# Attention feeding an ELU MLP on one core: q and k of each pair prepared two half slots sooner, and the first batch's x copied one half slot later

## The chip, the core and the metric

The kernel runs on one core of one Trainium2 chip. The metric is the device time of one execution in microseconds (us), given as the median of three runs.

The engines that matter here, by the names of the profile: PE (TensorE, matmuls), DVE (VectorE), ACT (ScalarE), POOL (GpSimd), and SP, whose queue issues every DMA of this kernel. Each engine takes its own instructions strictly in the order in which the program was written.

## What is computed

Eight batches of twelve heads, 448 positions, head size 64. q and k are RMS-normed with a gain, attention is plain softmax, and the heads of a batch are put side by side as x, which goes through a two-layer MLP with an ELU.

```python
def rmsnorm(x, g):
    rms = np.sqrt(np.mean(x * x, axis=-1, keepdims=True) + 1e-06)
    return x / rms * g
q_n, k_n = (rmsnorm(q, g_q), rmsnorm(k, g_k))
scores = scale * np.matmul(q_n, k_n.transpose(0, 1, 3, 2))
attn = softmax(scores)                       # max, exp, sum + 1e-9, divide
x = np.matmul(attn, v)                       # then (3584, 768)
h = x @ w_in                                 # 768 x 2048
g = np.where(h > 0.0, h, np.exp(np.minimum(h, 0.0)) - 1.0)
return g @ w_out                             # 2048 x 768
```

## The kernel before, in words

Heads are worked on in pairs, six pairs to a batch, 48 in all. A pair's 896 query rows are seven chunks of 128. Every float32 operand is split into a high and a low float16 part, so that a product is two or three float16 matmuls.

**Time is written out in half slots.** The main loop runs `h` from -18 to 699. A pair has `HP` = 14 half slots, a batch `HB` = 84. In an even half slot one chunk gets its row maximum (`s_max`, DVE, L542), the chunk before it its `s_z` (POOL, L552), the one before that its `s_hi` (ACT, L566). In an odd one there is `s_exp` (ACT, L548), `s_rec` (DVE, L559) and `s_lo` (DVE, L571). PE gets one chunk's score matmuls `s_mm` (L535) every two half slots, into four banks `s`; a bank is free again when that chunk's `s_lo` is done. `s_tr` (SP, L581) issues the DMA transposes of the attention weights, `pt<-gall` in the first batch and `pt<-p` later. At r = 7 of the next pair (r is the half slot inside a pair, `h` modulo 14) `attend` (PE, L592) multiplies them with v into the bank `av`, 22 matmuls. `x_high` (ACT, L599) and `x_low` (DVE, L603) then copy `av` into x.

**Everything else is a task hung on a half slot** by `at(h, fn, ...)`, and `run_tasks` writes out a half slot's tasks behind its softmax instructions. Thus a number in the table below decides where in each engine's queue an instruction stands, and nothing else. The order in which PE's instructions are written depends on those softmax steps, on the weights and on the MLP; the tasks moved here have none on PE.

**q and k of a pair** pass through `load_qk` (SP, DMA into `nat`), `qk_square` (ACT, L362), `qk_sum` (DVE, L366), `qk_root` (ACT, L370 and L371), `qk_newton` (DVE, L377 to L381), `qk_norm` (POOL, L391), `k_high` (ACT, L400), `q_gain` (POOL, L405), `q_high` (ACT, L410), `k_low` (POOL, L414), `q_low` (POOL, L421), two DMA transposes `qk_transpose` into `qkt` (SP, L429), and `q_swap` (SP, L436), two DMAs that put the halves of q the other way round. Only then can `s_mm` of the pair run. From the third pair on, `qk_square` writes its scratch into the `qkt` buffer that the next pair will fill.

**The weights** are split while the first two batches run: `conv_in` for sixteen blocks of `w_in` (load, two ACT steps L224 and L225 into `wts` and `w32s`, a DVE join L230 and sign L256, column sums on PE L129, POOL `whi` L282, PE L289 and L290, ACT `wli` L293), then `conv_out` for `w_out`. v has its own POOL steps (`v_mult`, `v_high` L448, `v_low` L453, `v_shift` L459).

The MLP's matmuls (L677, L691) start at h = 92, some seven to a half slot, and go on behind the attention's end. Its weights' low parts come from DRAM again for each batch (`wls`, L666), and batches from the third on have v read once more for its maximum (`vscan`, L162).

Of the kernel before, what the change touches and what calls it, by code (L numbers as in the profile page):

```python
# [20 lines left out]
NPAIR = H // 2  # L21
# [11 lines left out]
def tile_attention_then_elu_mlp(ctx: ExitStack, tc: tile.TileContext, qk, v, v_scan, gg, w_in, w_out, out):  # L33
# [668 lines left out]
    def at(h, fn, *args):  # L702
        tasks.setdefault(h, []).append((fn, args))
# [15 lines left out]
    }  # L719
    for p in range(NP):  # L720
        hb = HP * (p - 1)
        steps = (-20, -14, -12, -10, -8, -4, -1, -1, 1, 4, 2)
        steps = early.get(p) or [hb + h for h in steps]
        for h, fn in zip(steps, (
            load_qk, qk_square, qk_sum, qk_root, qk_newton, qk_norm, k_high, q_gain, q_high, k_low,
            q_low,
        )):

            at(-3 if p == 2 and fn == load_qk else h, fn, p)
        for h, i in ((4 if p > 1 else 6, 0), (6 if p > 1 else 8, 1)):  # L730
            at(hb + h, qk_transpose, p, i)
        at(hb + 8, q_swap, p)
        h0 = HP * p
        for h, fn in ((-2, load_v), (9, v_mult), (10, v_high), (11, v_low), (12, v_shift)):
            at(h0 + h + (5 if (p == 0) == (h > 0) and p < 2 else 0), fn, p)
        at(h0 + 22, x_high, p)
        at(h0 + 23, x_low, p)
    for b in range(B):
        h0 = HB * (b - 1) + (66 if b > 1 else 48) if b else -5
        for i in range(VSC):  # L740
# [27 lines left out]
    for h in range(H0, LAST):  # L768
# [28 lines left out]
        p, r = divmod(h, HP)  # L797
# [15 lines left out]
    h = LAST - 1  # L813
# [49 lines left out]
```

## Time and profile before

| | |
|---|---|
| three runs | 1286.1 us median, 1285.51 to 1286.39 |
| the profiled execution | 1287.73 us, of which 1285.6 us is the span from the first to the last instruction and 2.1 us lies around it |
| busy in the span | PE 1191.8 us (93%), ACT 878.7 (68%), DVE 853.3 (66%), POOL 529.4 (41%) |
| mean granted TensorE clock | 0.970 of full |
| DMA | 219.22 MB, nearly all issued by SP |

The profile gives one execution's instructions with start and duration. "Idle before <- releaser" is the time in which an engine did nothing ahead of an instruction, with what ended it. An engine's idle time matters where PE in turn waits for it.

### The profile page before, as it was taken

To read this page: it belongs to the slowest core of one execution; us is meant where nothing else is said; L and a number is where in the kernel's file an instruction comes from. 1 tells how busy PE (TensorE), PEld (TensorE's weight loads), DVE (VectorE), ACT (ScalarE), POOL (GpSimd) and SP (SyncE) were. 2 spreads that over 40 slices of the span, in tenths; PEclk is the share of its full clock that TensorE was granted. 3 is DMA by queue.
4 is the path that set the end of the run, shared out by engine and by line. 5 is a ranking of instruction groups with operands and counts; after the bars stand their busy time and mean duration, and the time that the engine had idled before them with its cause. 6 is when DMAs were issued, how large, how long until landed. Compare 5 with 4: busy or idle time off the path is not lost.

```text
span 1285.6 us, 21501 instructions
## 1 busy us (share of the span) xinstructions
PE 1191.8 (93%) x6976; PEld 716.4 (56%) x6976; DVE 853.3 (66%) x1913; ACT 878.7 (68%) x1889; POOL 529.4 (41%) x843
## 2 busy tenths in 40 slices
PE   3676578889999999999999999999999999999998
PEld 1333234456655765576556665576557755666576
DVE  7878779886677557856677567856785668642310
ACT  6887778985788558855797478855886578743520
POOL 3675775665334333343344433434334334420000
PEclk9878679999999999999999999999999999999999
DMA  8999898899877897889787986799787977663011
GB/s 274 224 215 239 199 224 181 199 205 236 175 147 154 203 197 142 164 166 223 149 164 157 215 176 148 155 197 203 139 169 166 219 152 171 133 147 87 1 47 62
DMA packets 452560, 219.22 MB, mean 171 GB/s; under 512 B 408673, under 2 KB 428769, under 8 KB 452449
## 3 DMA queue, kind: packets, MB, share of 16 engines
q1 hardware_dynamic: 452448, 217.86, 78.2%
q8 instruction: 55, 0.90, 0.3%
q14 instruction: 57, 0.46, 0.1%
HBM read 93.52 MB, written 14.16 MB: 84 GB/s over the span
## 4 chain that ended last, share of the span: by engine, by line
PE 79%; ACT 6%; DVE 5%; POOL 4%; issue 3%; DMA 2%; SPq 0%; ACTq 0%; POOLq 0%; DVEq 0%
PE mo L691 32%; PE mo L677 30%; PE s L535 8%; PE av L592 7%; DMA pt<-p 2%; PE mo L289 1%; ACT w32s L225 1%; ACT wts L224 1%; POOL nat L391 1%; ACT s L548 1%; POOL whi L282 1%; DVE wts L230 1%; DVE gall L571 1%; DVE st L542 1%; DVE gall L632 1%
## 5 line engine op out<-in xcount | busy, mean ns | idle before, releaser
L677 PE MATMUL mo<-x,whi 128*128 128x448 f16 x1536 | 422.8, 352 | 5.0 <-DVE e L624 5.0
L691 PE MATMUL mo<-gall,whos 128*128 128x448 f16 x1536 | 422.8, 353 | 0.7 <-DVE gall L632 0.7
L542 DVE TENSOR_REDUCE st<-s 128x1 f32<-128x448 f32 x336 | 208.4, 620 | 176.2 <-PE s L535 175.4
L552 POOL TENSOR_SCALAR st<-st 128x1 f32<-128x1 f32 x336 | 77.3, 230 | 552.4 <-ACT s L548 544.5
L691 PE MATMUL mo<-gall,wls 128*128 128x448 f16 x768 | 271.9, 354 | 0.0
L677 PE MATMUL mo<-x,wli 128*128 128x448 f16 x768 | 270.9, 353 | 0.0
L566 ACT ACTIVATE p<-s,st 128x448 f16<-128x448 f32 x294 | 185.6, 631 | 119.2 <-DMA pt<-p 99.9
L691 PEld LDWEIGHTS <-whos 128*128 128x128 f16 x1536 | 221.6, 145 | 72.3
L548 ACT ACTIVATE s<-s,st 128x448 f32<-128x448 f32 x336 | 203.2, 605 | 61.4 <-DVE st L542 58.4
L535 PE MATMUL s<-qkt 128*128 128x448 f16 (+1 forms) x768 | 188.8, 365 | 53.3 <-DVE gall L571 39.3
L677 PEld LDWEIGHTS <-whi 128*128 128x128 f16 x1536 | 150.2, 98 | 143.1 <-issue 6.9
L571 DVE SCALAR_TENSOR_TENSOR p<-s,st,p 128x448 f16<-128x448 f32 x294 | 196.4, 668 | 30.5 <-ACT p L566 28.5
L691 PEld LDWEIGHTS <-wls 128*128 128x128 f16 x768 | 110.4, 144 | 43.0 <-issue 8.4
L535 PEld LDWEIGHTS <-qkt 128*128 128x128 f16 (+1 forms) x768 | 63.2, 101 | 124.3 <-issue 62.4
L632 DVE SCALAR_TENSOR_TENSOR gall<-e,gsc,gall 128x448 f16<-128x448 f32 x128 | 100.8, 787 | 24.4 <-ACT gall L629 24.2
L677 PEld LDWEIGHTS <-wli 128*128 128x128 f16 x768 | 75.1, 98 | 74.7 <-issue 7.5
L592 PE MATMUL av<-pt,vt 128*64 128x448 f16 x1056 | 113.0, 362 | 0.1
L629 ACT ACTIVATE gall<-e,gsc 128x448 f16<-128x448 f32 x128 | 85.1, 665 | 24.3 <-DVE e L624 24.3
L599 ACT ACTIVATE x<-av 128x448 f16<-128x448 f32 x48 | 26.1, 543 | 104.4 <-PE av L592 104.4
L620 ACT ACTIVATE e<-e,nisc,isc 128x448 f32<-128x448 f32 x128 | 96.9, 757 | 0.3
L616 ACT ACTIVATE e<-mo,sc 128x448 f32<-128x448 f32 x128 | 80.6, 630 | 22.3 <-PE mo L677 22.0
L624 DVE SCALAR_TENSOR_TENSOR e<-e,mo 128x448 f32<-128x448 f32 x128 | 78.5, 613 | 16.6 <-ACT e L620 11.9
(100 smaller groups left out, 1372.6 us busy)
## 6 DMA issues: line engine op xcount, KB each, us to landing
wls<-wl_d SPq DMA_DIRECT2D x48, 512.0 KB, 3.9
nat<-in_qk SPq DMA_DIRECT2D x48, 448.0 KB, 3.9
raws<-in_w_out SPq DMA_DIRECT2D x24, 512.0 KB, 4.4
qkt<-qkt SPq DMA_DIRECT2D x96, 112.0 KB, 2.4
out<-y SPq DMA_DIRECT2D x48, 224.0 KB, 2.9
vn<-in_v SPq DMA_DIRECT2D x38, 256.0 KB, 3.7
vscan<-in_v_scan SPq DMA_DIRECT2D x36, 224.0 KB, 3.9
whos<-in_w_in SPq DMA_DIRECT2D x10, 768.0 KB, 5.5
```

The source lines that it names most:

```text
L535: nc.tensor.matmul(ps[r0 : r0 + n, :S], lhs, qq[:, 1, h * S : h * S + S], start=(t == 0), stop=(t == 2),)
L542: nc.vector.tensor_reduce(out=st[:, 0:1], in_=pss[T][:, :S], axis=AX.X, op=ALU.max, negate=True)
L548: nc.scalar.activation(ps, ps, AF.Exp, bias=st[:, 0:1], accum_out=st[:, 1:2])
L566: nc.scalar.activation(p16[:, :S], pss[T][:, :S], AF.Copy, scale=stats[T][:, 2:3])
L571: nc.vector.scalar_tensor_tensor(out=p16[:, S:], in0=ps[:, :S], scalar=r, in1=p16[:, :S], op0=ALU.mult, op1=ALU.subtract)
L592: nc.tensor.matmul(av[64 * h : 64 * h + 64, :S], vt[p][:, j + NJ * i, h], pt[h][:, j, :], start=(k == 0), stop=(k == len(terms) - 1),)
L616: nc.scalar.activation(e, ph[:, :S], AF.Exp, scale=sc)
L620: nc.scalar.activation(e, e, AF.Identity, scale=isc, bias=nisc)
L629: nc.scalar.activation(g[:, 0], e, AF.Copy, scale=gsc)
L632: nc.vector.scalar_tensor_tensor(out=g[:, 1], in0=e, scalar=gsc, in1=g[:, 0], op0=ALU.mult, op1=ALU.subtract)
L677: nc.tensor.matmul(ph[:, :S], w[:, c, :], x[:, r, :], start=(c == 0 and i == 0), stop=last)
L691: nc.tensor.matmul(py[:, :S], w, g[:, r, :], start=(f == 0 and i == 0), stop=last)
```

## The change

The table `steps` has one number for each of the eleven steps from `load_qk` to `q_low`. `hb` is 14 times (pair - 1). From the third pair on (p = 2) every number but that of `load_qk` falls by two. The two transposes and the swap of those pairs also fall by two, written with `- (4 if p > 1 else 0)`: the transposes go from `hb + 4` and `hb + 6` to `hb + 2` and `hb + 4`, the swap from `hb + 8` to `hb + 6`. The first two pairs keep their places. In the first batch's first five pairs (p = 0 to 4) `x_high` and `x_low` go from h0 + 22 and h0 + 23 to h0 + 23 and h0 + 24.

```diff
-        steps = (-20, -14, -12, -10, -8, -4, -1, -1, 1, 4, 2)
+        steps = (-20, -16, -14, -12, -10, -6, -3, -3, -1, 2, 0)
         steps = early.get(p) or [hb + h for h in steps]
...
             at(-3 if p == 2 and fn == load_qk else h, fn, p)
-        for h, i in ((4 if p > 1 else 6, 0), (6 if p > 1 else 8, 1)):
-            at(hb + h, qk_transpose, p, i)
-        at(hb + 8, q_swap, p)
+        for h, fn, *i in ((6, qk_transpose, 0), (8, qk_transpose, 1), (8 if p < 2 else 10, q_swap)):
+            at(hb + h - (4 if p > 1 else 0), fn, p, *i)
...
-        at(h0 + 22, x_high, p)
-        at(h0 + 23, x_low, p)
+        d = int(p < NPAIR - 1)
+        at(h0 + 22 + d, x_high, p)
+        at(h0 + 23 + d, x_low, p)
```

PE's own order is the same in both. Three places show what the table does to the others.

On ACT at the program's start, around the weights' third block: `dgw` is the second block's scale, the square (`qkt<-nat`) is the third pair's, `wts` and `w32s` are the third block's first steps.

```order
 L371 ACTIVATE r_212<-ln 128x14
-L279 ACTIVATE dgw<-ident,ws 128x128 x2
+L279 ACTIVATE dgw<-ident,ws 128x128
+L362 ACTIVATE qkt<-nat 128x896
+L279 ACTIVATE dgw<-ident,ws 128x128
 L224 ACTIVATE wts<-whos 128x768
 L225 ACTIVATE w32s<-whos 128x768
-L293 ACTIVATE wli_104<-mo 128x384
-L362 ACTIVATE qkt<-nat 128x896
-L293 ACTIVATE wli_104<-mo 128x384
```

The square has moved ahead of the second `dgw` and of the third block's first two steps. Its `load_qk` still stands at h = -3, now one half slot ahead of it instead of three.

On ACT where the second pair's x is copied, about 82 us into the span before (L548 is `s_exp`, L293 a weight's `wli`, L566 `s_hi`):

```order
 L225 ACTIVATE w32s<-whos 128x768
 L566 ACTIVATE gall<-s,st 128x448
+L293 ACTIVATE wli_112<-mo 128x384
+L548 ACTIVATE s,st<-s,st 128x448
 L599 ACTIVATE x_122<-av 128x448
-L293 ACTIVATE wli_112<-mo 128x384
-L548 ACTIVATE s,st<-s,st 128x448
 L279 ACTIVATE dgw<-ident,ws 128x128
```

The copy has moved behind one `wli` and one `s_exp`.

On POOL at the same place (L448 and L453 are v's high and low part, L391 `qk_norm`, L405 `q_gain`, L552 `s_z`, L459 `v_shift`):

```order
 L448 TENSOR_SCALAR vt<-gall 128x512
-L391 TENSOR_TENSOR nat<-nat,r_796 128x896
 L453 TENSOR_TENSOR vt<-gall,vt 128x512
-L552 TENSOR_SCALAR st<-st 128x1
-L459 COPY vt<-vt 64x384 x2
 L405 TENSOR_TENSOR nat<-nat,gst 128x448
+L552 TENSOR_SCALAR st<-st 128x1
+L459 COPY vt<-vt 64x384 x2
 L282 TENSOR_SCALAR whi_98<-w32s,ws 128x768
```

The norm has left the stretch, to a place ahead of `v_mult` and the last `whi`; the gain has come in ahead of the `s_z`.

On SP at the end of the 23rd pair, before (`pt` is the attention weights' transpose, `qkt<-t` L429 q's and k's, `qkt<-qkt` L436 the swaps; `vscan`, `out` and `nat` are loads and a store):

```order
L162 DMA vscan<-in_v_scan 128x448
L581 DMA_TRANSPOSE pt<-p_6710 128x7x128
L581 DMA_TRANSPOSE pt<-p_6747 128x7x128
L656 DMA out<-y 128x448
L162 DMA vscan<-in_v_scan 128x448
L429 DMA_TRANSPOSE qkt<-t_6690 128x7x128
L162 DMA vscan<-in_v_scan 128x448
L429 DMA_TRANSPOSE qkt<-t_6690 128x7x128
L340 DMA nat<-in_qk 128x896
L581 DMA_TRANSPOSE pt<-p_6783 128x7x128
L581 DMA_TRANSPOSE pt<-p_6817 128x7x128
L436 DMA qkt<-qkt 64x896 x2
```

And the same place now:

```order
L162 DMA vscan<-in_v_scan 128x448
L581 DMA_TRANSPOSE pt<-p_6713 128x7x128
L429 DMA_TRANSPOSE qkt<-t_6657 128x7x128
L581 DMA_TRANSPOSE pt<-p_6750 128x7x128
L656 DMA out<-y 128x448
L162 DMA vscan<-in_v_scan 128x448
L429 DMA_TRANSPOSE qkt<-t_6657 128x7x128
L162 DMA vscan<-in_v_scan 128x448
L436 DMA qkt<-qkt 64x896 x2
L340 DMA nat<-in_qk 128x896
L581 DMA_TRANSPOSE pt<-p_6789 128x7x128
L581 DMA_TRANSPOSE pt<-p_6822 128x7x128
```

q's transpose now stands ahead of the pair's last `pt` transpose, and the two swaps ahead of the next pair's first two instead of behind them.

## Rows read from the trace of the kernel before

**Rows 1.** Windows: busy us of each engine in three stretches, granted clock, DMA.

```profile
core 0: us, PE busy (x) PEld busy (x) DVE busy (x) ACT busy (x) POOL busy (x), PEclk, DMA share, GB/s
56.50:175.00 118.50, 72.21 (x450) 34.57 (x448) 96.19 (x217) 92.31 (x206) 79.35 (x100) 0.74 0.93 216
175.00:300.00 125.00, 110.38 (x738) 62.64 (x739) 105.97 (x233) 105.33 (x221) 83.78 (x105) 0.99 0.92 204
300.00:1156.00 856.00, 855.90 (x4967) 523.27 (x4966) 580.76 (x1317) 601.90 (x1321) 334.00 (x591) 1.00 0.83 172
```

**Rows 2.** Waits from 56.5 to 175 us: total us, times, longest.

```profile
DVE st L559 <- POOL st L552: 9.9, 7, 1.9
...
PE s L535 <- DMA qkt<-qkt: 9.0, 5, 2.3
ACT x L599 <- PE av L592: 8.1, 5, 2.1
...
DVE x L603 <- ACT x L599: 4.4, 4, 1.3
```

**Rows 3.** Timeline of ACT at the start: start us, us, what [idle before <-releaser].

```profile
20.06 0.40 ACT L279 ACTIVATE dgw<-ident,ws 128x128 f32<-128x128 f32 x1 [2.24 <-DVE ws L138]
...
21.16 0.88 ACT L225 ACTIVATE w32s<-whos 128x768 int32<-128x768 uint32 x1
...
22.77 0.95 ACT L362 ACTIVATE qkt<-nat 128x896 f32<-128x896 f32 x1 [0.36 <-DMA nat<-in_qk]
...
24.00 0.60 ACT L548 ACTIVATE s<-s,st 128x448 f32<-128x448 f32 x1
```

**Rows 4.** Timelines of SP, DVE and PE in the same stretch.

```profile
17.73 0.43 SPq L340 DMA_DIRECT2D nat<-in_qk  x1
...
22.07 1.20 DVE L230 SCALAR_TENSOR_TENSOR wts<-wts,w32s 128x768 uint32<-128x768 uint32 x1 [1.45 <-ACT w32s L225]
...
30.85 0.57 PE L535 MATMUL s<-qkt 128*64 128x448 f16 x4 [3.98 <-DVE gall L571]
```

**Rows 5.** Timeline of ACT where the second pair's x is copied.

```profile
82.16 0.54 ACT L599 ACTIVATE x<-av 128x448 f16<-128x448 f32 x1 [1.61 <-PE av L592]
...
82.97 0.62 ACT L548 ACTIVATE s<-s,st 128x448 f32<-128x448 f32 x1
...
87.94 0.60 ACT L548 ACTIVATE s<-s,st 128x448 f32<-128x448 f32 x1
```

**Rows 6.** Timelines of POOL and DVE in that pair.

```profile
80.44 1.54 POOL L282 TENSOR_SCALAR whi<-w32s,ws 128x768 f16<-128x768 f32 x1 [1.81 <-DVE ws L138]
83.79 0.49 POOL L552 TENSOR_SCALAR st<-st 128x1 f32<-128x1 f32 x1 [1.81 <-ACT s L548]
...
84.94 1.69 POOL L391 TENSOR_TENSOR nat<-nat,r 128x896 f32<-128x896 f32 x1
...
87.83 0.19 POOL L552 TENSOR_SCALAR st<-st 128x1 f32<-128x1 f32 x1
...
88.05 0.16 DVE L559 RECIPROCAL st<-st 128x1 f32<-128x1 f32 x1 [1.79 <-POOL st L552]
```

**Rows 7.** Timeline of PE: attend of the second, third and fifth pair.

```profile
79.83 2.27 PE L592 MATMUL av<-pt,vt 128*64 128x448 f16 x22
...
102.79 2.48 PE L592 MATMUL av<-pt,vt 128*64 128x448 f16 x22
...
150.15 4.32 PE L592 MATMUL av<-pt,vt 128*64 128x448 f16 x22
```

**Rows 8.** SP's timeline and the chain that ended last, in the 23rd pair.

```profile
573.52 1.18 SPq L436 DMA_DIRECT2D qkt<-qkt  x2
...
586.40 2.96 SPq L581 DMA_TRANSPOSE pt<-p  x2
...
588.00 4.12 DMA pt<-p
...
592.16 2.27 PE av L592 x21
```

## The prediction

> **What bounds the kernel now.** I read the windows first. From 300 us until the attention ends PE is busy for 855.9 of 856.0 us [rows 1]: there every other engine's work is hidden, and a moved instruction can only cost something. Ahead of that PE has holes. From 56.5 to 175 us it is busy for 72.2 of 118.5 us, from 175 to 300 us for 110.4 of 125.0 [rows 1]. So what the change is worth must come from before 300 us, and whatever is won there shifts all that follows, since PE has no more holes to lose it in.
>
> The waits say who holds PE up in the earlier stretch. DVE waits 9.9 us for POOL's `s_z`, seven times; PE waits 9.0 us for the swapped q, five times, once a pair; ACT waits 8.1 us for `attend` ahead of the copy to x, five times, and DVE 4.4 us for that copy [rows 2]. All three belong to steps that the change moves. They are not additive: one engine's wait overlaps another's. ACT and DVE are both near full (92.3 and 96.2 of 118.5 us [rows 1]), so most of a hole that closes will be met by the next engine's queue.
>
> **The change part by part, first the start.** The third pair's square is written behind the first `dgw` now, and its data are not there yet. SP issues that `nat` load at 17.73 us [rows 4], and ACT's square waited for it until 22.77 us [rows 3]; neither is moved. In the old order ACT filled that time with the second `dgw` at 20.06 and the third block's two steps, of which L225 ends at 21.16 + 0.88 = 22.04 [rows 3]. In the new one ACT stands still until 22.77, then takes the square (0.95, the next instruction starting some 0.1 us before its end), the `dgw` (0.4), and the two steps (0.8 each in a row), which puts L225's end at about 22.8 + 0.85 + 0.3 + 1.6 = 25.5. That is 3.5 us later. DVE's join already waited for L225, 1.45 us until 22.07 [rows 4]; it goes to 25.6, and as DVE takes its queue in order the first row maximum goes behind it, and the first exponential from 24.00 [rows 3] to about 27.1. PE in turn already waits 3.98 us at 30.85 for a bank that `s_lo` frees [rows 4], so nothing on its side takes up the delay. What comes back: the square no longer stands between two `wli` at 22.77 (0.85), and the logarithm, the root and the Newton steps are done in ACT's and DVE's new waits. I give 1.0 us for these. Term one: +2.5 us. Its ends are 0 (if the later queue has this much slack, which the chain of PE, DVE and ACT waits does not show) and +3.5.
>
> **The copy to x.** In the second pair's case ACT is free at 82.16 - 1.61 = 80.55 and waits for `attend`, 79.83 + 2.27 = 82.10 [rows 5, 7]. One `wli` and one exponential now go first: 82.97 - 82.16 less the copy's 0.54 leaves about 0.4 for the one, and 0.62 for the other [rows 5]. Both fit the hole. The copy starts at 82.16 as before, and ACT goes on about 1.0 us sooner than it did. There are five such waits, 8.1 us in all with 2.1 the longest [rows 2]; four exceed 1.0 us, the first is about 0.9. Term two: -4 x 1.0 - 0.9 = -4.9 us. Its ends are 0, if DVE is late there instead, and -8.1, the whole wait.
>
> **POOL's stretch.** With the exponential at 80.9, POOL's `s_z` follows `whi` at 80.44 + 1.54 = 81.98 and not at 83.79 [rows 6]. Behind it the norm (1.69 us [rows 6]) has left and the gain, on half as many elements, has come in, so it takes at most as long. The second `s_z` therefore moves from 87.83 to 86.0 or sooner, and DVE, which waited 1.79 us until 88.05 [rows 6] and so was free at 86.26, does not wait any more. But PE's next banks hang on ACT too: ahead of the exponential that stood at 87.94 [rows 5] ACT now has the moved `k_high` and the next square, about 1.3 us in the queue, which eats what was won by then and gives it back after it. Walking this pair through with the rows' durations, I find the next `attend` at about 101.6 instead of 102.79 [rows 7], 1.2 us, of which 1.0 is term two. Term three: five pairs at 0.2, -1.1 us with the rounding. Its ends are 0 and -9.9, DVE's whole wait [rows 2]; I take a value near the lower end because in the pair that I walked ACT is the next to be late.
>
> **The swap.** PE's 9.0 us for it [rows 2] go, since the swap now stands 2 half slots sooner. I cost that at nothing beyond terms two and three: each time PE then waits for a bank that `s_lo` frees, and for that DVE must come through POOL's stretch.
>
> **From 175 us on.** The steps are the same, in another order. From 175 to 300 us ACT is busy for 105.3 of 125.0 us [rows 1] and no wait there is for a moved step: 0, give or take 1. Behind 300 us SP's queue matters. In the 23rd pair the last `pt` transpose is issued at 588.00, lands 4.12 us later, and `attend` stands at that very moment (592.16) [rows 8]: no slack. Now q's transpose goes ahead of it, an issue of 1.2 to 1.5 us going by the 2.96 us for two [rows 8]. Yet the two swaps, 1.18 us at 573.52 [rows 8], are gone from the same run of issues between one `attend` and the next, and SP issues there almost without a break, so both sides cancel: 0. Without that cover it costs 1.3 us a time, and by the code such a pair (the fifth of its batch, where `vscan` and `wls` share SP) comes six times.
>
> A rule of the Trainium skill speaks against this zero: by "DMA: Bandwidth & Descriptors", section "Queues, rings and completion order", each DMA engine takes its descriptors in ring order, so the last `pt` would also stand behind the bytes of q's transpose. By it the landing moves even if the issue does not, and the sum would rise by up to the 7.8 us of the third rival below. The 4.12 us to landing do not tell issue from queueing.
>
> **Sum.** +2.5 - 4.9 - 1.1 + 0 = -3.5 us. The profiled execution took 1287.7 us (span 1285.6), so 1284.2 for such a one; it stood 1.6 us above the median of 1286.1, which makes 1282.6 us for the median.
>
> **The rivals.**
> First: the clock. From 56.5 to 175 us the granted clock was 0.74 of full [rows 1], a mix of 1.2 and 2.4 GHz, with PE idle for 46 us of it. `attend` took 2.27 us at 79.83 and 4.32 at 150.15 [rows 7]. If shorter waits keep PE at 2.4 GHz, the two long `attend` before 175 us lose some 2 us each: 1282.6 - 4.1 = 1278.5. For it speaks that `attend` and the matmuls behind it are on the chain there; against it that PE still has most of its holes. The rule behind it is in the Trainium skill's "TensorE: Matmul & The Clock Gate", section "What's actually happening": idle throttles the clock, activity releases it. The rows agree in direction.
>
> Second: the gain doesn't come. ACT gets free sooner, and DVE (96.2 of 118.5 us busy [rows 1]) or the pair's last `pt` is late instead, so that half of terms two and three is left: 1286.1 + 2.5 - 3.0 = 1285.6. That the moved steps were hidden all along, so that nothing changes, ends at the same place.
>
> Third, on the other side: SP in the tight pairs. If q's transpose delays the last `pt` there by its own 1.3 us and the swaps' leaving doesn't advance it (SP waits for a `wls` buffer or an earlier landing just ahead), PE stops six times: 1282.6 + 7.8 = 1290.4. It decides from about 0.4 us a time, where the six together take the gain below 1 us. For it speaks the missing slack [rows 8]; against it that SP is held only by its own issues in most of that run.
>
> **How the numbers follow.** Forecast 0.48, own range 1280.0 to 1285.0; clock 0.13; no gain 0.24, from 1284 to 1289 as the start costs 1 to 3.5; tight pairs 0.15. The range of 8 in 10 goes from 1277.0, just past the clock's case, to 1290.0, which leaves out about half of the tight pairs' case above and the ends of terms two and three below. A measurement of this kernel tells a difference from about 0.2%, 2.6 us, that is below 1283.5 or above 1288.7. Faster: most of the forecast (0.38) and the clock, 0.51. Within: the rest of the forecast (0.10) and most of the second rival, 0.28. Slower: the tight pairs and the second rival's end, 0.21.
>
> **What would show it.** Right: ACT waits some 2 us for `nat` at 20 us, and the first exponential stands near 27; the waits of ACT for `attend` fall to well below half; PE's wait for the swapped q and DVE's for POOL's `s_z` nearly vanish between 56 and 175 us; `attend` of the fifth pair, at 150.15 before [rows 7], comes some 2.3 us sooner (four pairs at 1.2, less the start's 2.5); PE is full behind 300 us. Wrong: PE waits behind 300 us, ahead of the fifth pair's `attend` in a batch; or the pairs before 175 us stay as far apart as they were, with DVE named in the waits; or the start's delay is taken up within the first pair.

## The result, and the profile after

The changed kernel takes 1290.9 us (median of 9 runs, 1289.1 to 1292.8); the kernel before took 1286.5 on the same chip (9 runs). The ratio is 1.0034, 95% interval 1.0026 to 1.0043: slower by 4.4 us, where the prediction said 3.5 us faster and ended its range at 1290. The profiled execution took 1290.0 us, with a span of 1288.1: 0.9 under its median, where the one behind [rows 1] to [rows 8] lies 1.2 over the 1286.5. So the two traces show some 2.3 of the 4.4 us.

Windows of the changed kernel, the same stretches as [rows 1]:

```profile
core 0: us, PE busy (x) PEld busy (x) DVE busy (x) ACT busy (x) POOL busy (x), PEclk, DMA share, GB/s
56.50:175.00 118.50, 71.51 (x451) 35.88 (x451) 97.39 (x220) 93.96 (x209) 80.30 (x105) 0.77 1.00 224
175.00:300.00 125.00, 109.34 (x738) 61.50 (x737) 108.16 (x238) 104.87 (x220) 85.41 (x105) 0.98 0.91 204
300.00:1156.00 856.00, 855.73 (x4968) 523.16 (x4967) 582.40 (x1317) 601.10 (x1324) 336.70 (x590) 1.00 0.82 172
```

PE is full behind 300 us as before. In the first stretch every engine is about as busy as it was, though it now begins 7.7 us ahead of the first `attend`. What has changed are the waits. Here they are from 64.2 to 179.5 us, that is from the first `attend` to the sixth as in [rows 2]:

```profile
PE s L535 <- DVE gall L571: 31.7, 14, 4.8
...
DVE a_in L132 <- PE mo L129: 7.9, 5, 2.7
PE mo L289 <- ACT dgw L279: 6.7, 3, 3.1
...
ACT x L599 <- PE av L592: 4.3, 4, 1.8
...
DVE st L559 <- POOL st L552: 1.0, 2, 0.6
```

Three that have grown, in the kernel before (56.5 to 175 us):

```profile
PE s L535 <- DVE gall L571: 28.6, 16, 3.0
...
PE mo L289 <- ACT dgw L279: 3.4, 6, 0.7
...
DVE a_in L132 <- PE mo L129: 3.2, 4, 1.2
```

PE's 9.0 us for the swapped q are gone, DVE's 9.9 for `s_z` are 1.0, ACT's 8.1 for `attend` are 4.3. But PE's wait for the bank that `s_lo` frees has grown from 28.6 to 31.7, that for the weights' scale `dgw` from 3.4 to 6.7, and DVE's for the column sums from 3.2 to 7.9. In all the five pairs take 115.2 us where they took 118.3; the loss lies ahead of the first `attend`.

ACT at the start, where [rows 3] stood:

```profile
23.23 0.95 ACT L362 ACTIVATE qkt<-nat 128x896 f32<-128x896 f32 x1 [5.45 <-DMA nat<-in_qk]
...
25.16 0.88 ACT L225 ACTIVATE w32s<-whos 128x768 int32<-128x768 uint32 x1
...
27.59 0.61 ACT L548 ACTIVATE s<-s,st 128x448 f32<-128x448 f32 x1 [0.81 <-DVE st L542]
...
38.26 0.61 ACT L548 ACTIVATE s<-s,st 128x448 f32<-128x448 f32 x1 [1.75 <-DVE st L542]
```

The third pair's square waits 5.45 us for its data. The first exponential stands at 27.59, 3.6 us late; the fourth, at 38.26, is 6.0 late. The kernel before had it at 32.23, and on DVE the fourth row maximum (L542) stood ahead of the third pair's Newton steps (L377):

```profile
32.23 0.61 ACT L548 ACTIVATE s<-s,st 128x448 f32<-128x448 f32 x1 [0.95 <-DVE st L542]
```

```profile
31.59 0.61 DVE L542 TENSOR_REDUCE st<-s 128x1 f32<-128x448 f32 x1
32.12 0.94 DVE L377 SCALAR_TENSOR_TENSOR ss<-ss,r 128x14 f32<-128x14 f32 x2
```

DVE of the changed kernel in the same stretch, where [rows 4] had the join at 22.07:

```profile
26.06 0.96 DVE L230 SCALAR_TENSOR_TENSOR wts<-wts,w32s 128x768 uint32<-128x768 uint32 x1 [5.49 <-ACT w32s L225]
...
31.96 1.83 DVE L377 SCALAR_TENSOR_TENSOR ss<-ss,r 128x14 f32<-128x14 f32 x2
33.82 0.17 DVE L378 SCALAR_TENSOR_TENSOR r<-ss,r 128x14 f32<-128x14 f32 x1
...
37.62 0.61 DVE L542 TENSOR_REDUCE st<-s 128x1 f32<-128x448 f32 x1
```

DVE waits 5.49 us with nothing to do. The third pair's Newton steps now stand ahead of the fourth row maximum (L542 at 37.62; before, Newton came behind it), and the first two take 1.83 us where they took 0.94. PE's `attend` of the first, second, third and fifth pair:

```profile
64.27 2.63 PE L592 MATMUL av<-pt,vt 128*64 128x448 f16 x22
86.31 0.38 PE L592 MATMUL av<-pt,vt 128*64 128x448 f16 x1
...
109.58 2.27 PE L592 MATMUL av<-pt,vt 128*64 128x448 f16 x22
154.73 3.46 PE L592 MATMUL av<-pt,vt 128*64 128x448 f16 x22
```

The first was at 56.59, so the start has lost 7.7 us in this execution. By the fifth pair 4.6 us are left of it (150.15 in [rows 7]), by the last `attend` 2.5 (1171.99 against 1169.54), about what the two whole executions differ by. The chain in the 23rd pair, where [rows 8] had no slack:

```profile
588.69 2.65 PE mo L691 x14
591.34 0.38 PE s L535 x2
591.72 2.65 PE mo L691 x14
594.37 0.50 PE s L535 x4
594.87 2.08 PE av L592 x22
```

PE runs through. No `pt` transpose is in the chain any more, though q's transpose now goes ahead of the last of them: that one is issued at 590.51 and lands 3.36 us later, 1.0 us ahead of `attend`.

### The profile page after: what moved, and what is told of

It is laid out like the page before. It is cut to its first block, busy times and chain, and to the rows that moved or that the text cites. A ratio compares the mean times of both kernels' runs of the same rounds, so it can differ in the third digit from the quotient of the medians.

```text
span 1288.1 us, 21532 instructions
## 1 busy us (share of the span) xinstructions
PE 1191.4 (92%) x6976; PEld 716.8 (56%) x6976; DVE 855.9 (66%) x1913; ACT 876.5 (68%) x1889; POOL 531.3 (41%) x843
## 4 chain that ended last, share of the span: by engine, by line
PE 76%; DVE 7%; ACT 3%; DMA 2%; issue 2%; SPq 1%; POOL 1%; ACTq 0%; DVEq 0%; POOLq 0%
PE mo L691 31%; PE mo L677 30%; PE s L535 8%; PE av L592 7%; DMA pt<-p 1%; DVE wts L230 1%; DVE st L542 1%; DVE w32s L256 1%; DVE gall L632 1%; DVE p L571 1%; ACT s L548 1%; DVE e L624 0%; DVE gall L571 0%; ACT w32s L225 0%; ACT p L566 0%
## 5 line engine op out<-in xcount | busy, mean ns | idle before, releaser
L542 DVE TENSOR_REDUCE st<-s 128x1 f32<-128x448 f32 x336 | 208.4, 620 | 179.7 <-PE s L535 178.9
L552 POOL TENSOR_SCALAR st<-st 128x1 f32<-128x1 f32 x336 | 85.8, 255 | 563.9 <-ACT s L548 559.8
L566 ACT ACTIVATE p<-s,st 128x448 f16<-128x448 f32 x294 | 185.8, 632 | 109.2 <-DMA pt<-p 85.9
L548 ACT ACTIVATE s<-s,st 128x448 f32<-128x448 f32 x336 | 203.2, 605 | 65.3 <-DVE st L542 64.9
L632 DVE SCALAR_TENSOR_TENSOR gall<-e,gsc,gall 128x448 f16<-128x448 f32 x128 | 96.9, 757 | 29.0 <-ACT gall L629 28.9
```

The source lines that it names most:

```text
L542: nc.vector.tensor_reduce(out=st[:, 0:1], in_=pss[T][:, :S], axis=AX.X, op=ALU.max, negate=True)
L548: nc.scalar.activation(ps, ps, AF.Exp, bias=st[:, 0:1], accum_out=st[:, 1:2])
L552: nc.gpsimd.tensor_scalar(out=st[:, 1:2], in0=st[:, 1:2], scalar1=1e-9, scalar2=2.0**-7, op0=ALU.add, op1=ALU.mult)
L566: nc.scalar.activation(p16[:, :S], pss[T][:, :S], AF.Copy, scale=stats[T][:, 2:3])
L632: nc.vector.scalar_tensor_tensor(out=g[:, 1], in0=e, scalar=gsc, in1=g[:, 0], op0=ALU.mult, op1=ALU.subtract)
```

## The experiments

Every kernel was timed in turn with the kernel before (5 to 12 executions each), and each difference below is against that one's median from the same turns (1286.1 to 1287.0). The intervals are some 1 us to either side, so differences under 1 us tell little. The ratio is taken over all executions and not from the medians: for p2_old it makes -1.0 us where the medians lie 1.7 apart.

| kernel | us | against before | ratio, 95% interval |
|---|---|---|---|
| changed | 1290.9 | +4.4 | 1.0034 (1.0026 to 1.0043) |
| p2_old | 1284.5 | -1.7 | 0.9992 (0.9983 to 1.0002) |
| p2_load | 1286.9 | +0.7 | 1.0010 (1.0001 to 1.0019) |
| old_load | 1286.0 | -0.6 | 0.9992 (0.9982 to 1.0002) |
| p2_square_old | 1285.3 | -1.3 | 0.9991 (0.9982 to 0.9999) |
| p2_newton | 1287.0 | +0.6 | 1.0005 (0.9996 to 1.0014) |
| x_only | 1282.9 | -3.2 | 0.9977 (0.9968 to 0.9985) |
| steps_only | 1293.7 | +7.5 | 1.0063 (1.0050 to 1.0075) |
| x_later | 1282.1 | -4.5 | 0.9966 (0.9953 to 0.9978) |
| p3_front | 1287.1 | +0.7 | 1.0006 (0.9997 to 1.0015) |
| front_newton | 1283.6 | -3.4 | 0.9977 (0.9968 to 0.9986) |
| square_sum | 1284.3 | -2.7 | 0.9978 (0.9969 to 0.9987) |
| p3_newton | 1282.3 | -4.7 | 0.9964 (0.9952 to 0.9977) |
| newton_back | 1287.9 | +1.3 | 1.0016 (1.0006 to 1.0025) |
| one_sooner | 1290.9 | +4.4 | 1.0029 (1.0019 to 1.0040) |
| from9 | 1283.8 | -2.6 | 0.9980 (0.9970 to 0.9990) |
| late_only | 1282.6 | -3.9 | 0.9966 (0.9954 to 0.9978) |
| best | 1283.2 | -3.4 | 0.9976 (0.9967 to 0.9986) |

**The start.** p2_old gives the third pair its old table back:

```diff
+        if p == 2:
+            steps = (-20, -14, -12, -10, -8, -4, -1, -1, 1, 4, 2)
...
-            at(hb + h - (4 if p > 1 else 0), fn, p, *i)
+            at(hb + h - ((2 if p == 2 else 4) if p > 1 else 0), fn, p, *i)
```

> The changed kernel, but the third pair alone (p = 2) keeps the old places for all its steps, transposes and swap; the fourth pair and all later ones, and the copy to x, are as changed. Theory (start): the third pair's square, written ahead of the third weight block, stands before data that have not landed, and that and what it pushes make the first attend 7.7 us late. Then the first attend is back near 57 to 58 us, the five gaps to the sixth pair's attend keep most of their 3.1 us, and the time falls by 5 to 7.5 us below the changed kernel, to 1283.5 to 1286. Rival one (the fourth pair's square and the third pair's k_high at 45 to 51 us cost just as much): the first attend stays at 60 us or later and the time at 1288 or more. Rival two (a later start is mostly met further on by a wait that it shortens, so that the tail of the start is worth little): the first attend is back at 57 but the attend of the eleventh pair moves by less than 3 us against the changed kernel, and the time is 1288 or more.

The time falls by 6.1 us (from +4.4 to -1.7) and the first `attend` is back at 57.57: the theory holds in both, and the start's loss is 6.1 us (5.4 by the ratios). The five gaps behind it kept only 1.5 of their 3.1 us, not most, in one trace. ACT at the start of p2_old:

```profile
23.10 0.95 ACT L362 ACTIVATE qkt<-nat 128x896 f32<-128x896 f32 x1 [0.75 <-DMA nat<-in_qk]
...
24.32 0.60 ACT L548 ACTIVATE s<-s,st 128x448 f32<-128x448 f32 x1
```

p2_load leaves the steps and moves the load:

```diff
-            at(-3 if p == 2 and fn == load_qk else h, fn, p)
+            at(-6 if p == 2 and fn == load_qk else h, fn, p)
```

> The changed kernel with one edit: the third pair's load of q and k is written at half slot -6 instead of -3, so that it is issued at about 13.3 us instead of 17.7. Theory (start, the wait for the data is the cause): the data land near 19 us, the square waits about 1.5 us instead of 5.45, the first exponential is back near 24 us and the time falls by 3 to 5 us, to 1286 to 1288; the part of the 7.7 us that other moved steps add later (some 3 us) stays. Rival (the order of the steps on ACT and DVE is the cause, not the data): the first exponential comes sooner but the first attend stays at 63 us or later, and the time stays above 1289. Rival two (the load pushes the first pair's transposes and the weights' loads back by as much): the first s_mm is later and nothing is won, 1290 or more.

The square stands at 17.49 and doesn't wait, the first exponential is back at 24.32, and 3.7 us come back, as the theory said. The first `attend` stays late, at 60.47. The load itself costs something: it goes ahead of a transpose of the first pair. old_load has the same edit on p2_old, where nobody needs the load sooner:

> The kernel with the third pair's old table (the fourth and later pairs and the copy as changed), with one edit: the third pair's load is written at half slot -6 instead of -3. There the load is needed by nobody sooner, so this measures what the early load itself costs. Theory (issued between the first pair's two transposes, it pushes the second transpose and the swap, so that the s_mm that stood at 18.7 us comes at 20 us or later): the first attend is 1 to 2.5 us later than 57.6 and the time 1285.5 to 1287, so that of what the early load left of the start's loss most was the load's own. Rival (the load is cheap): 1284 to 1285 and the first attend below 58.2 us; then what was left is due to the order of the third pair's steps.

1.1 us dearer than p2_old (the intervals overlap), first `attend` at 59.63: as the theory said. The first matmul that needs the swapped q, at 18.69 in p2_old, waits in p2_load until 20.16:

```profile
18.69 0.53 PE L535 MATMUL s<-qkt 128*128 128x448 f16 x1 [0.70 <-DMA qkt<-qkt]
```

```profile
19.11 0.53 PE L535 MATMUL s<-qkt 128*128 128x448 f16 x1 [2.13 <-DMA qkt<-t]
20.16 0.53 PE L535 MATMUL s<-qkt 128*128 128x448 f16 x1 [0.52 <-DMA qkt<-qkt]
```

If the early load costs the changed kernel as much, the wait for the data is worth about 3.7 + 1.1 = 4.8 of the 6.1 us. p2_square_old puts the third pair's square, sum, root and Newton steps back, without moving the load:

```diff
+        if p == 2:
+            steps = (-20, -14, -12, -10, -8, -6, -3, -3, -1, 2, 0)
```

> The changed kernel with the third pair's square, sum, root and Newton steps back at their old places; its norm, k_high, gain, high and low parts, transposes and swap stay as changed, and its load is not moved. So the square no longer stands before data that have not landed, and nothing else of the start is given up. Theory (the front half, that is the wait for the data and Newton's place, makes nearly all of the start's loss): the time is that of the kernel with the third pair's whole old table, 1284.5, give or take 1, and the first attend at 57 to 58.5 us. Rival (the moved k_high and gain of the third pair, ahead of softmax steps at 40 to 46 us, make some 2.5 us of it): the first attend at 59.5 to 61 us and the time at 1286.5 or more.

5.7 of the 6.1 us come back: those four steps are the loss. The norm and the back half (`k_high` to the swap) make the other 0.4, less than the intervals tell. Its profiled execution was the slowest of its runs, with the first `attend` at 59.77, past the theory's 58.5, so the medians carry this one. p2_newton tried to split these steps further. On top of p2_load it puts the root and Newton back:

```diff
+        if p == 2:
+            steps = (-20, -16, -14, -10, -8, -6, -3, -3, -1, 2, 0)
```

> The changed kernel with the third pair's load at half slot -6 as in the run before, and with that pair's root and Newton steps back at their old places; all else as changed. With the early load alone the fourth exponential stood at 34.4 us against 32.2 with the third pair's old table, and the first attend at 60.5 against 57.6. Theory (Newton's small steps, now ahead of a join and a row maximum on DVE and stretched while POOL works, make the most of that): the fourth exponential is back at 32.2 to 33 us, the first attend at 58 to 59, and the time falls by 1.5 to 2.5 us to 1284.3 to 1285.4. Rival (the third pair's k_high and the fourth's square on ACT at 43 us make it): the fourth exponential comes sooner, but the first attend stays at 60 us or later and the time at 1286.3 or more.

A miss for the theory. The fourth exponential came at 33.85, not below 33, the first `attend` stayed at 60.31 and the time at 1287.0. These are the rival's numbers, but they don't show its cause: in old_load the early load alone has the first `attend` at 59.63. Behind the early load, Newton's place at the start is worth nothing that shows (+0.6 and +0.7); newton_back, below, asks the same of the late start.

**The copy to x.** x_only is the kernel before with the last lines of the diff alone, steps_only the changed kernel with `d = 0`.

> The kernel before, with the later copy to x in the first batch as the only edit. Theory (the prediction's term two): ACT's wait for attend ahead of the copy falls by 3 us or more between 56 and 175 us, and the sixth pair's attend and the time come up to 4.9 us sooner, 1281.5 to 1284. Rival (what ACT wins there is met by the next queue, DVE or POOL): the wait falls, but the sixth pair's attend moves by less than 1.5 us and the time stays within 1.5 us of the kernel before. Rival two (the copy's later place delays the join x - x_high on DVE and so the row maximum): the time rises by 1 us or more.

> The changed kernel with the copy to x at its old place: only q's and k's steps, transposes and swaps are moved. Theory (start delay of 7.7 us, some 3 us won back by both edits in the five pairs behind it): the first attend is near 64 us as in the changed kernel, and the time is that of the changed kernel plus what the copy's later place is worth, 1 to 3 us: 1292 to 1294. Rival one (the copy is worth its predicted 4.9 us and the moved steps cost in the five pairs): 1295 or more. Rival two (the copy is worth nothing): within 1 us of the changed kernel.

Both theories' times came, and they agree: the copy is worth -3.2 us on the old table and -3.1 on the new one (4.4 - 7.5). (In steps_only the first `attend` stands at 61.27 and not near 64; the last section shows the clock's part in that.) In x_only ACT waits for `attend` for 2.5 us where it was 8.1. Two of the waits from the first to the sixth `attend`, and the second pair's copy in ACT's timeline:

```profile
PE s L535 <- DMA qkt<-qkt: 12.3, 5, 3.3
...
ACT x L599 <- PE av L592: 2.5, 3, 1.2
```

```profile
79.06 0.49 ACT L293 ACTIVATE wli<-mo 128x384 f16<-128x384 f32 x1
79.43 0.62 ACT L548 ACTIVATE s<-s,st 128x448 f32<-128x448 f32 x1
...
80.04 0.56 ACT L599 ACTIVATE x<-av 128x448 f16<-128x448 f32 x1
```

The `wli` and the exponential fill the hole, and the copy follows without a wait. x_later moves the copy one half slot further:

```diff
-        d = int(p < NPAIR - 1)
+        d = 2 * int(p < NPAIR - 1)
```

> The kernel before with the copy to x in the first batch two half slots later instead of one, and no other edit. With one half slot ACT still waited 2.5 us for attend (three times) between the first and the sixth attend, 8.1 before. Theory (the gain ends with ACT's wait; what is left of it can still be had): 1 to 2 us below one half slot, 1281 to 1282. Rival (PE's column sums on the bank of av wait for the copy and the difference, so that another half slot moves the wait there): 1283.5 to 1287.

-4.5 us, 1.3 more than one half slot, with ACT's wait at 0.7 us. The intervals overlap.

**The moved steps from the fourth pair on.** p2_old (-1.7) has them, x_only (-3.2) doesn't: they cost 1.5 us where the prediction's third term said -1.1. p3_front moves only the front half:

```diff
+        if p == 2:
+            steps = (-20, -14, -12, -10, -8, -4, -1, -1, 1, 4, 2)
+        if p > 2:
+            steps = (-20, -16, -14, -12, -10, -6, -1, -1, 1, 4, 2)
...
-            at(hb + h - (4 if p > 1 else 0), fn, p, *i)
+            at(hb + h - (2 if p > 1 else 0), fn, p, *i)
```

> The later copy to x as in the changed kernel, the third pair with its old table, and from the fourth pair on only the steps from the square to the norm moved; k_high, the gain, the high and low parts, the transposes and the swap stand at their old places. With all of them moved from the fourth pair on the time was 1284.5, with none 1282.9. Theory (the square, the Newton steps and the norm cost, since they stand ahead of softmax steps on ACT, DVE and POOL ahead of 175 us): 1284 to 1285.5. Rival (k_high and the gain ahead of the exponential and s_z cost): 1282.3 to 1283.5, and the gap ahead of the second attend is back near 20 us. Rival two (the swap standing sooner is what wins behind 175 us): the gap ahead of the tenth attend is 28.5 us, not 26.5, and the time is above 1285.5.

3.9 us above x_only, more than the theory expected. The second rival's time came as well, but the gap ahead of the tenth `attend` is 27.2 us, between its 28.5 and 26.5. The groups of DVE's instructions by line, from 57 to 175 us, show what has become dear. Newton's first line (busy us, mean ns) in x_only, in p3_front, in the changed kernel (64.2 to 179.5 us), and its first two lines in p2_old (57.5 to 174.5 us):

```profile
L377 DVE SCALAR_TENSOR_TENSOR ss<-ss,r 128x14 f32<-128x14 f32 x10 | 1.7, 166 | 0.2
```

```profile
L377 DVE SCALAR_TENSOR_TENSOR ss<-ss,r 128x14 f32<-128x14 f32 x10 | 7.3, 730 | 0.2
```

```profile
L377 DVE SCALAR_TENSOR_TENSOR ss<-ss,r 128x14 f32<-128x14 f32 x10 | 3.4, 335 | 0.2
```

```profile
L377 DVE SCALAR_TENSOR_TENSOR ss<-ss,r 128x14 f32<-128x14 f32 x10 | 2.8, 277 | 0.2
L378 DVE SCALAR_TENSOR_TENSOR r<-ss,r 128x14 f32<-128x14 f32 x5 | 1.7, 343 | 0.2
```

In p3_front the same ten instructions take 7.3 us instead of 1.7. Its timeline shows why:

```profile
71.78 1.04 POOL L414 TENSOR_TENSOR t<-nat,t 128x448 f16<-128x448 f32 x1
71.86 1.87 DVE L377 SCALAR_TENSOR_TENSOR ss<-ss,r 128x14 f32<-128x14 f32 x2
72.80 0.91 POOL L282 TENSOR_SCALAR whi<-w32s,ws 128x768 f16<-128x768 f32 x1
73.76 0.17 DVE L378 SCALAR_TENSOR_TENSOR r<-ss,r 128x14 f32<-128x14 f32 x1
```

The second of the two steps ends at 73.73, as POOL's second instruction ends at 73.71, and the first at 72.84, as POOL's first ends at 72.82; the third, with POOL idle, takes 0.17 us. The Trainium skill says in "SBUF — State Buffer", section "Who interferes with whom", that a DVE instruction with two SBUF inputs contends with a GpSimd (POOL) instruction that reads SBUF, and that the port pair they share is an exclusive lock. These rows agree. front_newton puts Newton alone back in p3_front, square_sum moves nothing but the square and its sum, p3_newton puts Newton alone back in p2_old:

```diff
+            steps = (-20, -16, -14, -12, -8, -6, -1, -1, 1, 4, 2)
...
+            steps = (-20, -16, -14, -10, -8, -4, -1, -1, 1, 4, 2)
...
+            steps = (-20, -16, -14, -12, -8, -6, -3, -3, -1, 2, 0)
```

> As the run with the front half of the steps moved from the fourth pair on (1287.1 us, 3.9 above the copy alone), but with Newton's steps back at their old place there; square, sum, root and norm stay moved. Theory (Newton beside POOL's work makes the loss): Newton's first two steps take 0.17 to 0.3 us each between 57 and 175 us instead of 0.73, and the time falls by 2 us or more, to 1283 to 1285. Rival (the square and its sum make it): Newton's steps get short, but the time stays at 1286 or more.

> The later copy to x, the third pair's old table, and from the fourth pair on only the square and its sum one half slot pair sooner; all else at the old places. Theory (Newton's place makes the loss): 1282.3 to 1283.8, as the copy alone. Rival (the square makes it): 1285.5 to 1287.5.

> The later copy to x, the third pair's old table, and from the fourth pair on all steps moved but Newton's, which stand at their old place. With Newton moved too the time was 1284.5. Theory (with Newton out of POOL's way the moved steps win what the prediction's third term said, or at least stop costing): 1281.5 to 1283.2, and Newton's first two steps below 0.3 us each. Rival (the waits that the swap's earlier place frees go to other engines anyway): 1284 to 1285.5.

Newton's place is the cause. Put back, it gives 4.1 us in front_newton and 3.0 in p3_newton, and there L377 takes 167 and 170 ns. square_sum lies 0.5 us above x_only, within the intervals, though just past its theory's range. That the longer steps alone are the loss is not shown. In p3_front they are longer by 5.6 us in five pairs and cost 4.1; in p2_old, by the two lines above, by 1.9 us (1.7 and 0.9 us in x_only), where 3.0 were lost. What else Newton's place does to DVE's queue no run separates. The rest of the moved steps is then worth -4.7 + 3.2 = -1.5 us, with overlapping intervals. newton_back does the same in the changed kernel, third pair and all:

```diff
-        steps = (-20, -16, -14, -12, -10, -6, -3, -3, -1, 2, 0)
+        steps = (-20, -16, -14, -12, -8, -6, -3, -3, -1, 2, 0)
```

> The changed kernel with one number put back: Newton's steps of the third and all later pairs stand at their old place. Theory (Newton's place costs 3 us behind the third pair and less than 1 at the start; the wait for the data stays): 1286.5 to 1288, and the first attend still at 62 to 64.5 us. Rival (at the start Newton beside POOL is most of the loss, the wait for the data is not): 1283 to 1285, and the first attend below 60 us. Rival two (with the start late, Newton's place costs nothing more): 1290 to 1291.

The theory came: 1287.9 us, 3.1 below the changed kernel, with the first `attend` still at 62.79. That is no more than the 3.0 of the later pairs, so that Newton's place at the start is worth about nothing. What is left against p3_newton, 6.0 us, is the third pair's other steps with the wait for the data. Nor is the start clear of POOL without Newton. A weight's sign step on DVE, 0.94 us in the kernel before (at 30.72), now runs beside POOL's `k_low` (34.75 to 35.78) and takes longer:

```profile
34.79 1.81 DVE L256 SCALAR_TENSOR_TENSOR w32s<-whos,wts 128x768 uint32<-128x768 uint32 x1
```

one_sooner is x_only with the back half alone one half slot sooner from the fourth pair on, which takes PE's wait for the swap from 12.3 to 2.7 us:

```diff
+        steps = (-20, -14, -12, -10, -8, -4, -2, -2, 0, 3, 1) if p > 2 else (-20, -14, -12, -10, -8, -4, -1, -1, 1, 4, 2)
...
+            at(hb + h - (p > 2), qk_transpose, p, i)
+        at(hb + 8 - (p > 2), q_swap, p)
```

> The kernel with the later copy alone, and from the fourth pair on the back half of the steps (k_high, gain, high and low parts, transposes, swap) one half slot sooner; square, sum, root, Newton and norm stay. With the copy alone PE waits 12.3 us for the swapped q between the first and sixth attend; with all steps two half slots sooner that wait was 2.0 us, but the waits for s_lo's bank, for the weights' diagonal and the column sums rose by as much, and the time was 1.5 us higher. Theory (the wait for the swap stands beside others, so that taking it away is worth nothing): 1282.3 to 1283.6, with PE's wait for the swap down to 8 us or less. Rival (the swap is the bound, and only the front half's earlier place cost): 1279.5 to 1281.5.

A miss for both: 7.6 us above x_only. The sixth `attend` is only 1.5 us late (171.66 against 170.13); most is lost from there to the tenth, 122.4 us instead of 114.8. There ACT now waits for `w_out`'s blocks, in the waits from 171 to 294 us:

```profile
ACT wts L224 <- DMA raws<-in_w_out: 7.8, 4, 4.2
```

It was 0.5 us in x_only. SP issues those loads too. Whether the moved transposes hold them up, and which, was not tried, so the cause of this loss stays open.

**Behind 175 us.** from9 and late_only keep the old table up to the ninth and the thirteenth pair (`p < 9`, `p < 13` in p2_old's condition).

> The later copy to x as in the changed kernel, and q's and k's steps moved only from the tenth pair on (p of 9 and more); pairs before keep the old table. In the trace with the copy alone the sixth to eleventh attend took 138.0 us, in those with the moved steps 135.8 to 136.7, nearly all of it in the gap ahead of the tenth attend. Theory one (the moved steps win some 2 us there by themselves, and cost only ahead of 175 us): the gap ahead of the tenth attend falls from 28.5 to 26.5 us and the time to 1280.5 to 1281.5, below the copy alone (1282.9). Rival (the win there is only the return of what the start lost, since PE had fallen behind): the gap stays at 28.5 and the time at 1282.3 to 1283.6.

> The later copy to x as in the changed kernel, and q's and k's steps moved only from the fourteenth pair on (p of 13 and more), so that the moved steps act behind 330 us alone, the tight pairs included. Theory (PE is full there, all of it is hidden): the time of the copy alone, 1282.3 to 1283.6. Rival (q's transpose ahead of the last pt in the tight pairs stops PE five times): 1285 or more. Rival two (the moved swaps take away small waits that PE had ahead of the 24th and the 42nd attend): 1281.8 to 1282.3.

late_only lies with x_only (-3.9 and -3.2), as its theory said: behind 330 us the moved steps cost nothing, in the tight pairs either. from9 is a miss for both. There the gap ahead of the tenth `attend` does fall, from 28.5 to 26.5 us, but the next two rise, from 23.2 to 23.8 and from 23.3 to 24.5, and the time is no better. From the eighth `attend` to the twelfth it wins 103.9 - 103.3 = 0.6 us.

**Together.** best is p3_newton with the copy two half slots later.

> The third pair with its old table, the later pairs with all steps moved but Newton's, and the copy to x in the first batch two half slots later. With the copy one half slot later and the same table it was 1282.3; the second half slot was worth up to 0.9 us with the old table. Theory (the two add up): 1280.8 to 1282. Rival (they win on the same waits): 1282 to 1283.5.

They don't add up, as the rival had it: -3.4 us. p3_newton (-4.7) and x_later (-4.5) are the fastest found, both below either kernel, and not told apart.

## Why the prediction was wrong

From the kernel before to the changed one there is a chain of kernels, x_only, p3_newton, p2_old, changed, so that the differences add up by construction:

| step | predicted | measured, from |
|---|---|---|
| copy one half slot later | -4.9 | -3.2, x_only less before |
| steps from the fourth pair on, Newton left out | -1.1, with Newton | -1.5, p3_newton less x_only |
| Newton from the fourth pair on | not priced | +3.0, p2_old less p3_newton |
| third pair's steps (the start) | +2.5 | +6.1, changed less p2_old |
| sum | -3.5 | +4.4 |

By the ratios the four are -3.0, -1.7, +3.6 and +5.4 us.

**Term one failed most**: 2.5 us was said, with an upper end of +3.5, and 6.1 measured. The mechanism was right: the square waits for data that is not moved, and the first exponential stands at 27.59 where 27.1 was said. But the delay at one instruction was taken as the most that could come of it, and 1.0 us was taken off for the square's old place and for the logarithm, the root and Newton "in ACT's and DVE's new waits". Those steps need the square, so they come behind the wait and not in it: DVE stood idle for 5.49 us, and Newton then went ahead of the fourth row maximum. By the fourth exponential 3.6 us had become 6.0. p2_square_old puts 5.7 us on the square, sum, root and Newton, the two load experiments 4.8 on the wait for the data. Newton is the smaller part of that growth. From the first to the fourth exponential it takes 8.2 us in the kernel before, 10.7 in the changed one and still 9.9 in newton_back, which has Newton behind the row maximum again. Which step makes the rest, and how the delay becomes 6.1 us of the time, stays open.

**Term three** failed at "walking this pair through with the rows' durations". No row there is one of Newton's, and the walk gave its new place no price. It cost 3.0 us, with steps that last longer beside POOL's work (0.17 us each before, 0.34 on average in the changed kernel's L377). Without Newton the term is -1.5 us, near the -1.1 that was said, but not clear of noise. No run moves the swap alone. Moved with the rest of the back half it won 1.3 us with Newton back (front_newton to p3_newton, intervals overlapping) and 2.4 with Newton moved (p3_front to p2_old). So most of its 9.0 us of wait were worth nothing, much as was said: PE then waited for `s_lo`'s bank and for `dgw`.

**Term two** was mis-sized: 1.0 us a pair was said, 0.6 measured (3.2 for five), with the mechanism as described.

**From 175 us on: 0** was right behind 300 us, and the third rival with it refuted: PE is busy for 855.73 of 856.00 us, with one wait of 0.2 us for a `pt`. The rule of the Trainium skill that was set against this zero ("DMA: Bandwidth & Descriptors", section "Queues, rings and completion order") thus made no price: the last `pt` of the 23rd pair landed 3.36 us after its issue, 4.12 in [rows 8]. From the eighth to the twelfth `attend` the moved steps gave 0.6 us in from9's trace, within the 1 that was allowed. **The clock** stood at 0.77 in the stretch against 0.74, and the fifth pair's `attend` got 0.9 us shorter; that is far from the 4.1 us, and with one trace each it may be chance. Of the two long `attend` in that rival's sum only the fifth pair's stands ahead of 175 us. **The second rival** had the direction for terms two and three: of their 6.0 us it left 3.0, and p2_old keeps 1.7. It was wrong to leave the start at 2.5. Its upper end of 1289 needs nearly all of the gain gone: with 3.0 us won, a start of 3.5 gives 1286.6.

Of the signs, the first exponential, the vanished waits for the swap and for `s_z`, and the full PE came as said. ACT's wait for `nat` came, but as 5.45 us and not some 2: the 2.24 us that ACT had waited ahead of the second `dgw` [rows 3] are now part of it. ACT's wait for `attend` fell by half, not to well below, and the fifth `attend` came 4.6 us later instead of 2.3 sooner.

## What to carry to other kernels

When a step is moved ahead of its data, the steps that depend on it are late by the same wait: price them where they then stand in the next engine's queue, and not in the hole. A moved instruction's duration is that of its new neighbours: a step of 0.17 us became one of 0.73 on average beside another engine's work (p3_front). And a wait that vanishes (here 9 us of PE for the swap) is worth only what the next one leaves.

## What the runs showed of the hardware

Kernels with one and the same order arrive at different times, as TensorE's clock happens to stand. x_only and from9 differ only behind 170 us. In both PE works at the lower level until 72.7 us (four matmuls of scores in 1.68 us), waits 1.86 us for `s_lo`'s bank and goes on at 74.5 with the same 23 matmuls. Windows from there to the second `attend`, in x_only and in from9:

```profile
74.50:77.20 2.70, 2.62 (x23) 1.48 (x22) 2.60 (x9) 1.87 (x6) 1.09 (x3) 1.00 1.13 336
```

```profile
74.50:79.50 5.00, 5.00 (x23) 2.51 (x22) 3.16 (x9) 3.38 (x7) 1.64 (x3) 0.50 1.13 252
```

The granted clock is 1.00 (2.4 GHz) in the one and 0.50 (1.2 GHz) in the other, and the second `attend` comes at 77.27 and at 79.56, 2.3 us apart. In the changed kernel and in steps_only, which have the same order up to the first `attend`, the same number of matmuls ahead of it takes:

```profile
59.10:64.20 5.10, 5.01 (x23) 2.54 (x22) 2.61 (x6) 3.01 (x7) 3.42 (x5) 0.50 1.22 270
```

```profile
58.50:61.20 2.70, 2.62 (x23) 1.48 (x22) 2.70 (x6) 1.25 (x5) 1.22 (x4) 1.00 1.07 252
```

Hence 64.27 in the one and 61.27 in the other, and a part of the 7.7 us that the first trace shows. What tips the clock to either side there, no run shows. By the sixth `attend` x_only and from9, still with the same order, are 3.9 us apart (170.13 and 174.04). A single trace ahead of 175 us can't carry a difference of 2 to 4 us in this kernel; the medians can.
